# Twenty-one small loads, read by nobody, beside the K and V loads of a one-token attention kernel

## The chip, the cores and the metric

The kernel runs on one core of a Trainium2 chip. The metric is the device time of one execution in microseconds. Several executions are timed and the median is taken; one more is recorded by the hardware profiler, and the traces are from that one. The engines of the core are TensorE (PE in the profile, PEld for its weight loads), VectorE (DVE), ScalarE (ACT), GpSimd (POOL) and SyncE (SP). SP does no arithmetic here: it issues DMAs. Sixteen DMA engines move the data between the chip's main memory (HBM) and the core's on-chip memory.

## The reference

One new token is decoded. Part A is attention of 32 query heads over a cache of 8 key/value heads, each with 32768 positions of 128 bf16 values. Part B is a gated feed-forward block of width 1792. A scalar gate mixes the two.

```
def _A_ref(x, k_cache, v_cache, wq, wo):
    q = (x @ wq) as [B, 32, Sq, 128];  k, v = each cache head repeated 4 times
    scores = einsum("bhqd,bhkd->bhqk", q, k) * (Dh ** -0.5)
    p = softmax(scores)
    o = einsum("bhqk,bhkd->bhqd", p, v)
    return o as [B, Sq, 4096] @ wo

def _B_ref(x, w_gate, w_up, w_down):
    return (silu(x @ w_gate) * (x @ w_up)) @ w_down

g = sigmoid((x * gate_w).sum(-1))
return g * A + (1 - g) * B
```

Here B = Sq = 1 and D = 512. The K and V caches hold 8 x 32768 x 128 bf16 values each, 134 MB together, out of 148 MB that the kernel reads.

## The kernel before, in words

The program is written engine by engine, with semaphores between the engines; the order on each engine is the order of the code, and there is no scheduler.

**The pages.** On-chip memory holds five pages (`page`, each 128 partitions x 32 KB, 4.2 MB), called A, B, C, V and F in the code (PG_A to PG_F; the V loads use the last two). The K cache of one head takes two pages (A and B, or B and C, by turns), the V cache of one head the other two. So there is room for the K of one head, half of the next, and the V of one.

**SyncE's order** (lines 303 to 363, function `_(sp)`). It issues wq (line 340), w_gate and w_up (342), then the K loads of heads 0 and 1 in halves (320), and from head 2 on one load of 8.4 MB for each head (311). Between them stand the V loads (335): K of head g, then V of head g-1. A K load waits until PE has read half of the K pages of the head before (`sem_fill`), a V load until PE is done with the V pages of the head before (`sem_v_free`). The last V load goes into the K pages. Behind them come w_down (350, tile `wd`, and 358 for its rest, which waits for a memset by GpSimd on line 301), and the output weights wo in five pieces (363). SyncE's DMAs go through one queue, q1 in the profile.

**PE** has a loop over the 8 heads. `emit_k` (lines 391 to 415) brings each K page into PSUM by transposes (line 371, tile `pst`), VectorE copies the result into on-chip memory (line 765, tile `ktT`), and PE multiplies it with the queries (line 383, `ps_sc`). Then the maximum is taken (420, 424), ScalarE computes the exponentials (633, tile `ET`), and `emit_v` multiplies them with the V pages of the head before (line 440, `ps_o`). After the loop come the last head's V, w_down, and wo (lines 235 and 246).

**GpSimd** (lines 276 to 301) makes a few constants, and then relays the arrival of the K pages. PE waits on two semaphores for the two halves of a head's K. For heads 0 and 1 two DMAs raise them; from head 2 on one DMA raises only the first, `sem_k[0]`. So GpSimd waits for it and raises the second:

```
                for g in range(1, G):
                    pool.wait_ge(sem_k[1], 16 * g)
                    if g > 1:
                        pool.wait_ge(sem_k[0], 16 * (g + 1))
                    else:
                        pool.wait_ge(sem_k1, 16)
                    pool.sem_inc(sem_k[1], 16)
```

PE asks for the second semaphore before the second half of a head, after the eight transposes of the first half. GpSimd issues no DMA in this version. The kernel's end is the store of the output in two halves, issued by SyncE and ScalarE (line 270); SyncE then waits for both (line 822).

Of the kernel before, what the change touches and what calls it, by code (L numbers as in the profile page):

```python
# [8 lines left out]
BF16 = mybir.dt.bfloat16  # L9
# [3 lines left out]
def bass_gated_mix__gqa_block_cached__swiglu_ffn__decode_kernel(  # L13
# [61 lines left out]
    NPG = 5  # L75
    assert G % 2 == 0
    PAD = 768

    XH, XE, XQ, FX = 2, 4, 4, 4
    XP = XE * XQ  # L80
# [6 lines left out]
    with ExitStack() as es:  # L87
        def S_(name):
            return es.enter_context(nc.semaphore(name))
# [10 lines left out]
        sem_ld_wd = S_("s_ld_wd")  # L100
        sem_ld_wx = S_("s_ld_wx")
        sem_wz = S_("s_wz")
        sem_ones = S_("s_ones")
        sem_dc = S_("s_dc")
        sem_pz = S_("s_pz")
# [42 lines left out]
        def T(name, shape, dt):  # L148
            return es.enter_context(nc.sbuf_tensor(name, shape, dt))
# [18 lines left out]
        tX = T("tX", [XS, FX], BF16)  # L168
        pad = T("pad", [128, PAD // 2], BF16)
        page = T("page", [128, NPG, PAGE], BF16)  # L170
# [14 lines left out]
        O2a = T("O2a", [128, WOJ], BF16)  # L185
        O2 = T("O2", [128, WOJ], BF16)
        res_row = T("res_row", [128, 128], BF16)

        def P(name, shape, dt):
            return es.enter_context(nc.psum_tensor(name, shape, dt))  # L190
# [78 lines left out]
        def emit_store(eng, half, rows):  # L269
            eng.dma_start(  # L270
                out[0, 0, 256 * half : 256 * (half + 1)].rearrange("(c n) -> c n", c=2),
                rows[31 + 64 * half : 33 + 64 * half, :],
            ).then_inc(sem_out, 16)

        with nc.Block("main") as block:
            @block.gpsimd
            def _(pool):
                pool.memset(ones_f[:, :], 1.0).then_inc(sem_ones, 1)
                pool.memset(ones_bf[:, :], 1.0).then_inc(sem_ones, 1)
                pool.memset(r_row[:, 0, 0:1], 0.0).then_inc(sem_r, 1)  # L280
                n, k = 1, 1
                while n < 128:
                    pool.wait_ge(sem_r, k)
                    pool.tensor_scalar(
                        r_row[:, 0, n : 2 * n], r_row[:, 0, 0:n], float(n), None, op0=ALU.add
                    ).then_inc(sem_r, 1)
                    n *= 2
                    k += 1
                pool.wait_ge(sem_r, k)
                pool.tensor_scalar(  # L290
                    r_row[:, 1, :], r_row[:, 0, :], -1.0, None, op0=ALU.mult
                ).then_inc(sem_r, 1)
                for g in range(1, G):
                    pool.wait_ge(sem_k[1], 16 * g)
                    if g > 1:
                        pool.wait_ge(sem_k[0], 16 * (g + 1))
# [3 lines that stand above are left out]
                pool.wait_ge(sem_fill, UPG * G)  # L300
                pool.memset(wz, 0.0).then_inc(sem_wz, 1)  # L301

            @block.sync
            def _(sp):
                def load_k(g):
                    lo = PG_A if g % 2 else PG_B
                    dst = page[:, lo : lo + NB, :].rearrange("p b (r d) -> p b r d", d=DH)
                    src = A_k_cache[0, g, :, :].rearrange("(p b r) d -> p b r d", b=NB, r=R)
                    if g > 1:
                        sp.wait_ge(sem_fill, UPG * (g - 1) + UPP)  # L310
                        sp.dma_start(
                            dst.rearrange("p b r d -> p (b r d)"),
                            src.rearrange("p b r d -> p (b r d)"),
                        ).then_inc(sem_k[0], 16)
                        return
                    for b in range(NB):
                        first = lo + b == PG_B
                        if g and first:
                            sp.wait_ge(sem_fill, UPP)
                        sp.dma_start(dst[:, b, :, :], src[:, b, :, :]).then_inc(  # L320
                            sem_k[0] if first else sem_k1 if g else sem_k[1], 16
                        )

                def load_v(g):
                    src = A_v_cache[0, g, :, :].rearrange("(p b r) d -> p b r d", b=NB, r=R)
                    if g == G - 1:
                        lo, sem = PG_L, sem_vl
                        sp.wait_ge(sem_fill, UPG * g + UPP)
                    else:
                        lo, sem = PG_V, sem_v  # L330
                        if g:
                            sp.wait_ge(sem_v_free, STEP * (g + 1))
                        else:
                            sp.wait_ge(sem_pe_h, 1)
                    sp.dma_start(
                        page[:, lo : lo + NB, :].rearrange("p b n -> p (b n)"),
                        src.rearrange("p b r d -> p (b r d)"),
                    ).then_inc(sem, 16)

                sp.dma_start(wq_v, A_wq.rearrange("(p c) n -> p c n", c=KC)).then_inc(sem_q, 16)  # L340
                for w, src in enumerate((B_w_gate, B_w_up)):
                    sp.dma_start(
                        wgu[:, w, :, :], src.rearrange("(p c) f -> p c f", c=KC)
                    ).then_inc(sem_f, 16)
                load_k(0)
                for g in range(1, G):
                    load_k(g)
                    load_v(g - 1)
                load_v(G - 1)
                sp.dma_start(  # L350
                    wd[:, :, :], B_w_down[0:FR, :].rearrange("(p j) n -> p j n", j=FM)
                ).then_inc(sem_ld_wd, 16)
                sp.wait_ge(sem_wz, 1)
                rest = B_w_down[FR:F, :].rearrange(
                    "(h q e i) n -> h e q (i n)", h=XH, q=XQ, e=XE
                )
                for h in range(XH):
                    sp.dma_start(wx[h], rest[h]).then_inc(sem_ld_wx, 16)
                sp.wait_ge(sem_v_free, STEP * G)
                src = A_wo.rearrange("(p j) n -> p j n", j=WOJ)  # L360
                for k, s in enumerate(sem_wo):
                    a, b = WO_CUTS[k], WO_CUTS[k + 1]
                    sp.dma_start(wo_v[:, a:b, :], src[:, a:b, :]).then_inc(s, 16)  # L363
# [445 lines left out]
        pe, act, dve, sp = nc.tensor, nc.scalar, nc.vector, nc.sync  # L809
# [9 lines left out]
        for half, eng in enumerate((sp, act)):  # L819
            eng.wait_ge(sem_dve_row, 1)  # L820
            emit_store(eng, half, res_row)
        sp.wait_ge(sem_out, 32)


# [26 lines left out]
```

## Time and profile before

| | |
|---|---|
| median of 3 runs | 349.11 us (349.1 to 349.25) |
| profiled execution, its own time | 349.16 us |
| span of its trace, first to last instruction | 347.8 us |
| mean granted clock of TensorE | 0.851 of full speed |
| read from HBM | 148.11 MB, 426 GB/s over the span |

How to read the views: times are microseconds from the span's start, unless marked ns. L371 is line 371 of the kernel. A tile's name followed by an arrow shows what is written from what. In a list of waits the columns are: who waited, for whom, microseconds in total, how often, the longest. In a timeline or a chain they are: start, duration, what. A DMA instruction on "SPq" shows the time that SyncE needs to issue it, and not the transfer. A large load is many packets, spread over the 16 DMA engines; when an engine has done its part of a load, it writes its count to a semaphore, a packet of 4 bytes. The answers on DMA packets count the packets that start in the window which the text names; "under 2 KB" includes those under 512 B.

### The profile page before, as it was taken

To read this page: it belongs to the slowest core of one execution; us is meant where nothing else is said; L and a number is where in the kernel's file an instruction comes from. 1 tells how busy PE (TensorE), PEld (TensorE's weight loads), DVE (VectorE), ACT (ScalarE), POOL (GpSimd) and SP (SyncE) were. 2 spreads that over 40 slices of the span, in tenths; PEclk is the share of its full clock that TensorE was granted. 3 is DMA by queue.
4 is the path that set the end of the run, shared out by engine and by line. 5 is a ranking of instruction groups with operands and counts; after the bars stand their busy time and mean duration, and the time that the engine had idled before them with its cause. 6 is when DMAs were issued, how large, how long until landed. Compare 5 with 4: busy or idle time off the path is not lost.

```text
span 347.8 us, 8869 instructions
## 1 busy us (share of the span) xinstructions
PE 260.8 (75%) x3925; PEld 220.6 (63%) x3925; DVE 186.6 (54%) x232; ACT 33.4 (10%) x143; POOL 4.6 (1%) x16
## 2 busy tenths in 40 slices
PE   1354995999749982999459982999469972999475
PEld 1124994998449941997259942996269842996232
DVE  3144995698119931697129921895149820895101
ACT  1002000300130003000300003000400012000400
POOL 3000000000000000000000000000000000002000
PEclk9996999699659987699959985898869985898669
DMA  8999999999999999999999999999999999999996
GB/s 322 419 459 426 420 422 458 469 414 437 414 430 475 415 437 415 437 467 415 437 407 445 467 414 437 407 452 460 414 437 407 452 460 415 437 407 452 406 418 261
DMA packets 3946, 148.21 MB, mean 426 GB/s; under 512 B 450, under 2 KB 580, under 8 KB 868
## 3 DMA queue, kind: packets, MB, share of 16 engines
q1 hardware_dynamic: 3932, 148.11, 98.7%
q8 instruction: 6, 0.10, 0.1%
q10 hardware_dynamic: 8, 0.00, 0.0%
HBM read 148.11 MB, written 0.00 MB: 426 GB/s over the span
## 4 chain that ended last, share of the span: by engine, by line
DMA 64%; PE 33%; DVE 2%; issue 1%; SPq 1%; ACT 0%; DVEq 0%
DMA page<-in_A_k_cache_dram 52%; PE pst L371 24%; DMA page<-in_B_w_up_dram 6%; DMA page<-in_A_wo_dram 6%; PE ps_sc L383 5%; PE ps_o L440 2%; PE pst L535 1%; DVE ktT L722 1%; DVE ktT L765 0%; SPq L363 0%; PE ps_m L553 0%; PE ps_m L566 0%; DVE ktT L712 0%; DVE ktT L710 0%; PE ps_sc L246 0%
## 5 line engine op out<-in xcount | busy, mean ns | idle before, releaser
L765 DVE COPY ktT<-pst 128x2048 bf16<-128x2048 bf16 x128 | 153.3, 1221 | 64.6 <-PE pst L371 60.4
L371 PE MATMUL pst<-ident_f,page 128*128 128x128 f32 x1024 | 147.2, 299 | 39.5 <-DMA page<-in_A_k_cache_dram 38.2
L371 PEld LDWEIGHTS pst<-ident_f,page 128*128 128x128 f32 x1024 | 126.0, 154 | 43.9 <-DMA page<-in_A_k_cache_dram 38.8
L383 PE MATMUL ps_sc<-qcur,ktT 128*128 128x8 bf16 x2048 | 64.1, 166 | 6.3 <-DVE ktT L765 6.3
L383 PEld LDWEIGHTS ps_sc<-qcur,ktT 128*128 128x128 bf16 x2048 | 63.8, 97 | 8.0 <-DVE ktT L765 7.1
L440 PE MATMUL ps_o<-page,ET 128*16 128x512 bf16 x512 | 39.4, 477 | 5.5 <-DMA page<-in_A_v_cache_dram 5.5
L440 PEld LDWEIGHTS ps_o<-page,ET 128*16 128x16 bf16 x512 | 15.0, 107 | 26.1 <-issue 18.8
L633 ACT ACTIVATE ET<-ps_sc,nbias 128x128 bf16 x64 | 23.9, 555 | 49.9 <-DVE nbias L791 49.9
L626 ACT ACTIVATE acc<-ps_o 128x512 f32<-128x512 f32 x8 | 4.8, 597 | 223.8 <-PE ps_o L440 218.9
L783 DVE TENSOR_REDUCE gm<-ps_m 4x1 f32<-4x128 f32 x8 | 2.2, 279 | 40.6 <-PE ps_m L420 40.6
L633 ACT ACTIVATION_READ_ACCUMULATOR ET<-ps_sc,nbias 128x1 f32 x64 | 18.3, 285 | 0.0
L773 DVE TENSOR_REDUCE pmaxf<-ps_sc 128x4 f32<-128x512 f32 x16 | 11.0, 686 | 8.4 <-PE ps_sc L383 8.4
L497 PE MATMUL pst<-page,xT 128*1 128x512 bf16 x32 | 3.6, 627 | 8.9 <-DMA page<-in_A_wq_dram 8.9
L461 PE MATMUL ps_m<-sel,acc 128*128 128x4 f32 x64 | 8.4, 255 | 1.8 <-ACT acc L626 1.6
L461 PEld LDWEIGHTS ps_m<-sel,acc 128*128 128x128 f32 x64 | 7.7, 191 | 2.5 <-ACT acc L626 2.2
L424 PE MATMUL ps_m<-diag,ones_f 4*128 4x4 f32 x16 | 3.8, 306 | 6.8 <-DVE diag L787 6.8
L424 PEld LDWEIGHTS ps_m<-diag,ones_f 4*128 4x128 f32 x16 | 3.3, 259 | 8.4 <-issue 8.4
L750 DVE RECIPROCAL rS<-ps_m 128x4 f32<-128x4 f32 x9 | 1.6, 182 | 12.2 <-PE ps_m L461 12.2
L497 PEld LDWEIGHTS pst<-page,xT 128*1 128x1 bf16 x32 | 0.9, 115 | 10.7 <-issue 10.7
L685 DVE CAST ktT<-pst 128x1024 bf16<-128x1024 f32 x2 | 2.4, 1220 | 8.2 <-PE pst L497 8.2
L452 PEld LDWEIGHTS ps_m<-esum,ones_f 128*128 128x128 f32 x32 | 4.2, 190 | 3.5 <-issue 3.5
L301 POOL MEMSET page<- 48x2048 bf16 x1 | 1.8, 1798 | 311.7 <-PE pst L371 311.7
(76 smaller groups left out, 54.6 us busy)
## 6 DMA issues: line engine op xcount, KB each, us to landing
page<-in_A_k_cache_dram SPq DMA_DIRECT2D x4, 4096.0 KB, 34.9
page<-in_A_wq_dram SPq DMA_DIRECT2D x1, 4096.0 KB, 13.4
page<-in_A_wo_dram SPq DMA_DIRECT2D x1, 2048.0 KB, 17.4
page<-in_B_w_gate_dram SPq DMA_DIRECT2D x1, 1792.0 KB, 17.2
page<-in_B_w_up_dram SPq DMA_DIRECT2D x1, 1792.0 KB, 21.0
wd<-in_B_w_down_dram SPq DMA_DIRECT2D x1, 1664.0 KB, 30.3
page<-in_A_wo_dram SPq DMA_DIRECT2D x1, 1152.0 KB, 19.8
page<-in_A_wo_dram SPq DMA_DIRECT2D x1, 512.0 KB, 20.6
```

Of the source, the lines that this page charges most:

```text
L371: ins = pe.transpose(pst[u % NST][:, k * 128 : (k + 1) * 128], kv[:, n * 128 : (n + 1) * 128], ident_f[:, :],)
L383: ins = pe.matmul(ps_sc[b][:, col : col + 2 * HPG], kt[:, k, e, :], qcur[:, e, :], start=(e == 0), stop=(e == 1),)
L424: pe.matmul(ps_m[:, M_B0 : M_B0 + HPG], ones_f[0:HPG, :], diag[:, :], start=True, stop=True,).then_inc(sem_b, STEP)
L440: ins = pe.matmul(ps_o[32 * c : 32 * c + RQ * HPG, :], ET[:, n : n + RQ, :].rearrange("p n h -> p (n h)"), v[:, k * RQ : (k + 1) * RQ, :], ...
L452: pe.matmul(ps_m[:, M_S0 : M_S0 + HPG], ones_f[:, :], esum[:, b, :], start=(b == 0), stop=(b == NB - 1),)
L461: ins = pe.matmul(ps_m[:, M_P0 : M_P0 + HPG], acc[:, q, :], sel4[:, q * HPG : (q + 1) * HPG], start=(q == 0), stop=(q == RQ - 1),)
L497: ins = pe.matmul(pst[0][32 * k : 32 * k + 1, t * QN : (t + 1) * QN], xT[:, c : c + 1], wq_v[:, c, n : n + QN], start=(c == 0), stop=(c == ...
L535: ins = pe.matmul(pst[1][32 * k : 32 * k + 1, w * 512 : w * 512 + FS], xT[:, c : c + 1], wgu[:, w, c, k * FS : (k + 1) * FS], start=(c == ...
L626: act.activation(part, ps_o[:, :], ACT.Copy).then_inc(sem_acc, STEP)
L633: act.activation(ET[:, b * R : (b + 1) * R, h], sc[:, h, bass.ds(bank, R)], ACT.Exp, bias=nbias[:, h : h + 1], scale=SCALE, accum_out=esum ...
L765: dve.tensor_copy(ktT[:, n % NKT, :], pst[n % NST][:, :].bitcast(BF16)).then_inc(sem_cp, 1)
L773: dve.tensor_reduce(pmaxf[:, b, :], sc, AX.X, ALU.max).then_inc(sem_d, 1)
```

## The change

SyncE issues 15 additional loads (`load_mark`): one after each K load from head 1 on, and one after each V load. The first has 15 rows, the next 14, and so on down to one; a row is 128 bytes (64 bf16 values) of wq. GpSimd issues six loads just before it waits for the K pages of head 4: of 1, 1, 3, 5, 7 and 15 rows, with row lengths from 160 to 352 bytes. The tiles that they fill, `mark` and `turn0` to `turn5`, are read by nobody. At the end SyncE waits for both groups, ahead of the wait for the output's store. On each engine the other instructions stay as they were, in the same order.

```
--- before.py
+++ after.py
@@ -75,6 +75,8 @@
     PAD = 768
+    MARKS = list(range(15, 0, -1))
+    TURNS = [(1, 80), (1, 96), (3, 112), (5, 144), (7, 160), (15, 176)]
 
@@ -185,6 +189,8 @@
         res_row = T("res_row", [128, 128], BF16)
+        mark = T("mark", [16, len(MARKS), 64], BF16)
+        turn_t = [T(f"turn{i}", [16, n], BF16) for i, (_, n) in enumerate(TURNS)]
 
@@ -291,6 +297,9 @@
                 for g in range(1, G):
+                    if g == 4:
+                        for t, (k, n) in zip(turn_t, TURNS):
+                            pool.dma_start(t[0:k, :], A_wq[0:k, 0:n]).then_inc(sem_turn, 16)
                     pool.wait_ge(sem_k[1], 16 * g)
@@ -337,6 +346,13 @@
+                marks = list(enumerate(MARKS))
+
+                def load_mark():
+                    if marks:
+                        m, n = marks.pop(0)
+                        sp.dma_start(mark[0:n, m, :], A_wq[0:n, 0:64]).then_inc(sem_mark, 16)
+
@@ -345,8 +361,12 @@
                 for g in range(1, G):
                     load_k(g)
+                    load_mark()
                     load_v(g - 1)
+                    load_mark()
                 load_v(G - 1)
+                load_mark()
+                assert not marks
                 sp.dma_start(
@@ -819,6 +839,8 @@
             emit_store(eng, half, res_row)
+        sp.wait_ge(sem_mark, 16 * len(MARKS))
+        sp.wait_ge(sem_turn, 16 * len(TURNS))
         sp.wait_ge(sem_out, 32)
```

The two new semaphores, `sem_mark` and `sem_turn`, are made beside the others.

More of the change, by code (lines that the diff above doesn't have):

```diff
@@ L102, in bass_gated_mix__gqa_block_cached__swiglu_ffn__decode_kernel @@
         sem_wz = S_("s_wz")
+        sem_mark = S_("s_mark")
+        sem_turn = S_("s_turn")
         sem_ones = S_("s_ones")
```

## The prediction

> **What bounds the kernel now.** I began with the head of the page, the busy shares in slices and the table of the queues.
>
> ```profile
> span 347.8 us, 8869 instructions
> ...
> PE 260.8 (75%) x3925; PEld 220.6 (63%) x3925; DVE 186.6 (54%) x232; ACT 33.4 (10%) x143; POOL 4.6 (1%) x16
> ...
> DMA  8999999999999999999999999999999999999996
> ...
> q1 hardware_dynamic: 3932, 148.11, 98.7%
> q8 instruction: 6, 0.10, 0.1%
> ```
>
> The row of digits is the mean busy share of the 16 DMA engines: nine tenths or more in every slice but the first and the last. Nearly all of it is one queue, q1, SyncE's. PE is busy for 75% of the span and DVE for 54%, so neither of them is the bound as a whole. Next I read one long stretch with the view by windows (the columns end in DMA share and GB/s), and then the waits of PE.
>
> ```profile
> 48.00:320.00 272.00, 217.77 (x3366) 191.94 (x3368) 159.94 (x185) 24.55 (x118) 1.80 (x1) 0.85 1.00 434
> ```
>
> ```profile
> PE pst L371 <- DMA page<-in_A_k_cache_dram: 38.2, 7, 7.9
> ```
>
> In the 272 us between 48 and 320 the DMA share is 1.00 at 434 GB/s, or 27.1 GB/s for each engine. No engine pauses between one load and the next. PE waits for the K pages seven times, 38.2 us in all, and this is its longest wait by far. So the time is the number of bytes over the rate of the engines, plus a short start and a short end. A change pays or costs here if it makes an engine's queue run dry, if it adds to an engine's work, or if it makes the end longer.
>
> The issue times of the SyncE queue tell whether a queue can run dry. First the timeline of that engine, then its waits, then the median time from issue to landing.
>
> ```profile
> 43.95 0.33 SPq L320 DMA_DIRECT2D page<-in_A_k_cache_dram  x1
> 44.32 0.43 SPq L335 DMA_DIRECT2D page<-in_A_v_cache_dram  x1
> ```
>
> ```profile
> 73.44 0.33 SPq L311 DMA_DIRECT2D page<-in_A_k_cache_dram  x1
> 91.53 0.33 SPq L335 DMA_DIRECT2D page<-in_A_v_cache_dram  x1
> ...
> 305.73 0.43 SPq L350 DMA_DIRECT2D wd<-in_B_w_down_dram  x1
> 317.52 1.48 SPq L358 DMA_DIRECT2D page<-in_B_w_down_dram  x2
> ```
>
> ```profile
> SPq L311 <- PE pst L371: 130.6, 6, 28.7
> SPq L335 <- PE ps_o L440: 103.1, 6, 17.7
> ...
> SPq L335 <- PE pst L371: 22.8, 1, 22.8
> ```
>
> ```profile
> page<-in_A_v_cache_dram SPq DMA_DIRECT2D x8, 28.4
> ```
>
> A V load is 8.39 MB (8 heads of 32768 x 128 bf16, one head each). At 434 GB/s it streams for 19.3 us, but it lands 28.4 us after its issue. So it stands some 9 us in the queue behind the load before it. SyncE itself idles: it waits 130.6 us ahead of six K loads 103.1 us ahead of six V loads and 22.8 us ahead of the last V load.
>
> Last, what the engines look like at one landing. The K load issued at 189.38 lands near 216. These are three answers on the DMA packets, for 213.9 to 214.7, 214.7 to 215.3 and 215.3 to 216.0 us.
>
> ```profile
> DMA packets 20, 0.66 MB, mean 819 GB/s; under 512 B 10, under 2 KB 10, under 8 KB 10
> ```
>
> ```profile
> DMA packets 0, 0.00 MB, mean 0 GB/s; under 512 B 0, under 2 KB 0, under 8 KB 0
> ```
>
> ```profile
> DMA packets 12, 0.39 MB, mean 562 GB/s; under 512 B 6, under 2 KB 6, under 8 KB 6
> ```
>
> Loads are made of large packets, so the packets under 512 B are the closing semaphore writes, one for each engine: 10 + 0 + 6 = 16. Ten engines finish their share, then nothing closes for 0.6 us, then the other six finish. The engines run side by side without waiting for each other, and **the six late engines set each landing**. Up to 0.6 us of extra work on any of the ten early ones is free.
>
> **The change, part by part.** It removes nothing and moves nothing between engines: the instructions of PE, DVE and ACT are the same in both programs. SyncE gets 15 more DMA instructions, GpSimd six, and SyncE two more waits at its end.
>
> *Issue time on SyncE.* The prices are in the view by tile (columns: ns least, median, most).
>
> ```profile
> L335 SPq DMA_DIRECT2D page<-in_A_v_cache_dram x8: 327/328/432, 44.3 to 305.4; - x8
> L358 SPq DMA_DIRECT2D page<-in_B_w_down_dram x2: 641/712/784, 317.5 to 318.4; - x2
> ```
>
> A mark of few rows can be like either, so 15 marks take 15 x 0.33 = 4.9 us to 15 x 0.78 = 11.8 us of SyncE's time. I take 0.33, since a mark has a plain shape. Thirteen of them stand where SyncE then waits for PE for many microseconds, in the waits quoted above, and cost nothing. Two have an instruction right behind them that waits for nothing: the V load at 44.32 goes out at 44.7 to 45.1, and the wd load at 305.73 at 306.1 to 306.5. Both stand in the queue behind the rest of a load that was just issued (4.2 MB of K or 8.4 MB of V, 10 to 19 us of streaming), so neither is late. What comes after wd is held by GpSimd's memset until 317.52 anyway. Without that cover each would cost its 0.33 to 0.78 us.
>
> *Work on the DMA engines.* All marks go into SyncE's queue between the large loads, so each of their packets takes time on an engine that has no pause. The price of a small packet comes from the end of the kernel, where the last loads have short rows. This is the answer for 344.5 to 345.5 us.
>
> ```profile
> DMA packets 150, 0.18 MB, mean 184 GB/s; under 512 B 20, under 2 KB 100, under 8 KB 150
> ...
> q1 hardware_dynamic: 150, 0.18, 50.4%
> ```
>
> 50.4% of 16 engines in 1 us is 8.06 us of engine time. The 0.18 MB at 27.1 GB/s are 6.6 us. The other 1.4 us over 150 packets is about 10 ns for each packet, whatever its size (8 to 11 with the rounding of 0.18). A row of 128 B is then 10 + 4.7 = 15 ns and the semaphore write behind it 10 ns: 25 ns for each mark on each engine that it uses. The marks have 15 + 14 + ... + 1 = 120 rows, so an engine has 7.5 of them on average, at least 0 and at most 15: 0.19 us, between 0 and 0.37 us. An early engine hides even 0.37 us in its 0.6 us. No trace row tells which engines are the late ones, so I take the average for them.
>
> The Trainium skill, "DMA: Bandwidth & Descriptors", section "Why a DMA increments its semaphore by 16 and not by 1", says that a load of n rows from SyncE uses the largest divisor up to 16, and the lowest-numbered engines. By that page the lowest engine has all 15 marks and the highest none, and the sum would be 0.37 or 0 in place of 0.19; no view here numbers the engines.
>
> *GpSimd's six loads.* In the changed program the first two rows are cut into 16 pieces each, so there are 16 + 16 + 3 + 5 + 7 + 15 = 62 data packets, and up to 6 x 16 = 96 semaphore writes. 158 x 10 ns, and 10 KB at 27.1 GB/s (0.4 us), are 2.0 us over 16 engines: 0.12 us each. GpSimd's own time for them is in no trace of before. From below it is nothing. From above, its longest instruction is 1.80 us (the one in the row by windows), and six of those are 10.8 us. I take about 1 us each, for no sum depends on it: between the relay for head 3 and the need of the one for head 4 there is time, as these rows of the chain of waits show.
>
> ```profile
> 138.93 5.38 PE pst L371 x24
> ...
> 177.56 5.23 PE pst L371 x24
> ...
> 189.38 26.77 DMA page<-in_A_k_cache_dram
> ```
>
> PE begins on the K pages of head 3 at 138.93, and GpSimd can start its DMAs then. PE begins on head 4 at 177.56 and needs GpSimd's relay only for the second half of it, at about 189.4. That is 50 us of cover for 0 to 10.8 us.
>
> *The end.* The two waits are passed long before: the marks are complete when the wd load behind them is. They run beside the output's store.
>
> ```profile
> SPq L822 <- DMA out_dram<-res_row: 1.0, 1, 1.0
> ```
>
> **Sum:** 0.19 + 0.12 = 0.31 us more on the late engines, between 0 and 0.5. The profiled execution took 349.16 us (its span of 347.8 and 1.4 around it), which gives 349.47. The median of the runs is 349.11, and from there it is 349.42. I forecast **349.4 us**, 0.1% more. A measurement of this kernel can tell about 0.2%, 0.7 us, from no change, so this counts as the same. A gain has no source in the sum, as no engine gets less to do.
>
> **The rivals.**
>
> *A small load leaves a hole (slower).* The engine might pause until a mark's row is in, ahead of the next load's first packet. The least a small DMA takes from issue to landing is the 1.0 us of the store above. With 15 holes of 1.0 us on a late engine that is 15 us: 364. Against it stands the DMA share of 1.00 at all borders between loads; for it, that none of those borders has a packet of 128 B read between two large ones. It decides from 0.7 us on: 47 ns for each mark on an engine with 15, or 93 ns with 7.5. A mild hole of 0.1 us on 7.5 marks beside the sum gives 350.2. Chance 0.12, most of it below 351.
>
> The same page of the Trainium skill, section "Anatomy of one DMA — SWDGE (gpsimd) path", puts about 2 us of fixed cost on each DMA. By that figure 15 marks one after the other would be an estimated 30 us. The share of 1.00 speaks against paying it in a row.
>
> *GpSimd's relay comes late (slower).* Lines 293 to 299 forward the arrival of K pages. If the six DMAs hold GpSimd for more than 50 us, over 8.4 us each, PE starts the second half of head 4 late. The loads have about 9 us of cover more, so 10 us each, 60 in all, would be 1 us past both covers: 350.4. Nothing in the profile is near 8 us on GpSimd. Chance 0.02.
>
> The Trainium skill, "SBUF — State Buffer", section on the "DVE blocks DMA" trap, says that GpSimd cannot write its descriptors while some VectorE copies run. [...]
>
> *Another block of code is fetched (slower).* Queue q8 above is code: 6 packets of 16 KB, 0.1% of 16 x 347.8 us = 5.6 us, 0.9 us of one engine each. Six fetches and six late engines: a fetch seems to be what makes an engine late. If the added instructions bring one more and it falls on a late engine, that is 349.4 + 0.9 = 350.3. On an early engine it is largely hidden. 21 instructions are few beside 16 KB. Chance 0.08.
>
> *The late engines come out less late (faster).* A fetch that falls elsewhere changes who is last. At most the 0.6 us gap and some 0.3 go: 348.4. Nothing in the change aims there. Chance 0.03.
>
> That the loads are left out of the program is excluded: all 21 are in the instruction lists of the changed one.
>
> **How the numbers follow.** Forecast 0.75, holes 0.12, code 0.08, relay 0.02, less late 0.03. Faster by over 0.2% is 0.03, slower by over 0.2% is 0.12 + 0.08 + 0.02 = 0.22, the rest is 0.75. The forecast's own range is 349.0 to 349.7: its sum of 0 to 0.5 on 349.1, and the spread of the runs. With the fetch and the milder half of the holes, the range that holds 8 in 10 is 349.0 to 350.4.
>
> **What would show it.** The DMA share between 48 and 320 us stays at 1.00 and the K loads keep their period of some 38.6 us (138.93 to 177.56). SyncE's queue shows each mark at some 0.3 us and the V load of 44.32 some 0.4 us later, its landing unchanged. The gap between the two groups of engines stays, shifted by tenths. It is wrong if slices of the DMA row fall below 9, if queue q8 has more than 6 packets, or if PE waits for GpSimd ahead of L371.

## The result, and the profile after

The changed kernel takes 350.41 us (median of 5, 350.33 to 350.5) against 349.11 before: a ratio of 1.0036 with the interval 1.0021 to 1.005. It is 1.3 us slower, more than the 0.3 us of the forecast: 0.7 us above the forecast's own range (up to 349.7), and 0.01 us past the upper end of the range that was to hold 8 in 10 (350.4).

The page of the profile after, in the rows that bear on the prediction:

```profile
span 349.1 us, 8891 instructions
...
DMA  8999999999999999999999999999999999999995
...
DMA packets 4378, 148.24 MB, mean 425 GB/s; under 512 B 882, under 2 KB 1012, under 8 KB 1300
...
q1 hardware_dynamic: 4172, 148.13, 98.5%
q8 instruction: 6, 0.10, 0.1%
q0 software_dynamic: 192, 0.01, 0.0%
```

In the DMA row the first slice is 8 as before, the last is 5 where it was 6, and no slice between them has fallen below 9. The code queue q8 still has six packets, so no code was fetched anew. q1 has 4172 - 3932 = 240 packets more: 120 rows and 120 closing writes, so a mark of n rows used n engines. The new queue q0 is GpSimd's; its data is 10 KB. Its 192 packets are 62 of data, as the prediction had them, and 130 writes of 4 bytes, where it had up to 96.

Now the instructions that were added, in the timeline of SyncE and in that of GpSimd (start, duration, what).

```profile
45.47 0.48 SPq L354 DMA_DIRECT2D mark<-in_A_wq_dram  x1
46.00 0.35 SPq L344 DMA_DIRECT2D page<-in_A_v_cache_dram  x1
46.39 1.19 SPq L354 DMA_DIRECT2D mark<-in_A_wq_dram  x1
73.66 0.33 SPq L320 DMA_DIRECT2D page<-in_A_k_cache_dram  x1
...
306.04 0.29 SPq L354 DMA_DIRECT2D mark<-in_A_wq_dram  x1
306.37 0.33 SPq L370 DMA_DIRECT2D wd<-in_B_w_down_dram  x1
317.82 1.43 SPq L378 DMA_DIRECT2D page<-in_B_w_down_dram  x2
```

```profile
139.62 3.19 POOL L302 DMA_DIRECT2D turn<-in_A_wq_dram  x6 [135.60 <-POOLq L308]
```

SyncE issues a mark in 0.29 to 0.48 us, and one in 1.19, behind which it waits for PE anyway. GpSimd issues its six loads in 3.19 us, long before its relay is needed at 189.

Where does the time go, then? The chain of waits shows when PE starts on a head's K pages, that is, when they have landed.

```profile
100.33 4.38 PE pst L391 x24
111.35 27.61 DMA page<-in_A_k_cache_dram
139.01 5.31 PE pst L391 x24
150.92 27.50 DMA page<-in_A_k_cache_dram
189.66 27.43 DMA page<-in_A_k_cache_dram
217.14 5.38 PE pst L391 x24
...
255.79 4.96 PE pst L391 x24
...
324.98 21.79 DMA page<-in_A_wo_dram
...
347.42 0.29 DVE res_row L838
```

The same rows of before have these times:

```profile
100.32 4.61 PE pst L371 x24
...
138.93 5.38 PE pst L371 x24
...
151.10 26.42 DMA page<-in_A_k_cache_dram
...
216.20 4.70 PE pst L371 x24
...
254.84 4.38 PE pst L371 x24
...
346.19 0.29 DVE res_row L818
```

At 139 the two kernels are level (0.08 us apart). The K load of head 4 then lands 0.90 us late: 150.92 + 27.50 = 178.42, against 151.10 + 26.42 = 177.52. At 217 the changed kernel is 0.94 us late, at 255 still 0.95. So in this execution nearly all of the loss arises in one period, between the landings at 139 and 178, although marks are issued from 45 to 306 us. It is the period in which GpSimd's loads are under way; the last of them lands near 170 us. At the end the loss has grown to 1.23: the output's copy on VectorE starts at 347.42 instead of 346.19.

In that stretch the engines are nearly as busy as ever, but on longer packets. The answer on DMA packets for 143.9 to 146.3 us, first before, then after:

```profile
DMA packets 16, 1.05 MB, mean 437 GB/s; under 512 B 0, under 2 KB 0, under 8 KB 0
...
q1 hardware_dynamic: 16, 1.05, 100.9%
```

```profile
DMA packets 31, 0.98 MB, mean 410 GB/s; under 512 B 16, under 2 KB 16, under 8 KB 16
...
q1 hardware_dynamic: 15, 0.98, 100.2%
q0 software_dynamic: 16, 0.00, 0.4%
```

Before, 16 packets of 64 KB take 100.9% of 16 engines x 2.4 us: 2.42 us each. After, 15 take 100.2% of the same: 2.57 us each. The small packets of q0 take 0.4%, and the large ones beside them have become 6% longer in this window. (Whether 15 or 16 start in it depends in part on where it cuts; the duration of each does not.) **The share counts a held-up packet as busy**; the bytes and the duration of the large packets tell.

Each packet of the trace has a start and a duration, and sums over all of them give the whole account. After, the large packets took 0.36 us more on each engine than before. There are also real pauses, moments in which an engine has no packet: 4.3 us of engine time, 0.27 us for each engine; the trace before has none between 20 and 330 us. Most of them, 4.1 us, lie between 140 and 160 us; at 157 us five of the 16 engines stand still for 0.3 us. The additional small packets are 0.2 to 0.3 us for each engine. The three make 0.83 to 0.93, and near 306 us the large packets start 0.88 us later than before, on average over the engines. What is missing up to 1.25 is in the section on the prediction.

### The profile page after: what moved, and what is told of

Same layout as the page of the kernel before. It is cut to its first block, busy times and chain, and to the rows that moved or that the text cites. A ratio compares the mean times of both kernels' runs of the same rounds, so it can differ in the third digit from the quotient of the medians.

```text
span 349.1 us, 8891 instructions
## 1 busy us (share of the span) xinstructions
PE 258.4 (74%) x3925; PEld 218.8 (63%) x3925; DVE 186.5 (53%) x232; ACT 33.4 (10%) x143; POOL 7.8 (2%) x22
## 3 DMA queue, kind: packets, MB, share of 16 engines
q1 hardware_dynamic: 4172, 148.13, 98.5%
## 4 chain that ended last, share of the span: by engine, by line
DMA 59%; PE 34%; DVE 3%; issue 2%; SPq 1%; ACT 0%; DVEq 0%
DMA page<-in_A_k_cache_dram 47%; PE pst L391 25%; DMA page<-in_A_wo_dram 6%; PE ps_sc L403 6%; DMA page<-in_B_w_up_dram 6%; DVE ktT L785 2%; PE ps_o L460 1%; PE pst L555 1%; DVE ktT L742 1%; SPq L383 0%; PE ps_m L573 0%; PE ps_m L586 0%; DVE pmaxf L793 0%; DVE ktT L732 0%; DVE ktT L730 0%
## 5 line engine op out<-in xcount | busy, mean ns | idle before, releaser
L391 PE MATMUL pst<-ident_f,page 128*128 128x128 f32 x1024 | 146.6, 298 | 42.2 <-DMA page<-in_A_k_cache_dram 40.5
L391 PEld LDWEIGHTS pst<-ident_f,page 128*128 128x128 f32 x1024 | 125.5, 154 | 46.6 <-DMA page<-in_A_k_cache_dram 41.1
L460 PE MATMUL ps_o<-page,ET 128*16 128x512 bf16 x512 | 38.2, 465 | 6.4 <-DMA page<-in_A_v_cache_dram 6.4
L460 PEld LDWEIGHTS ps_o<-page,ET 128*16 128x16 bf16 x512 | 14.2, 105 | 26.6 <-issue 18.8
L302 POOL DMA_DIRECT2D turn<-in_A_wq_dram x6 | 3.2, 538 | 135.6 <-POOLq L308 135.6
```

The source lines that it names most:

```text
L391: ins = pe.transpose(pst[u % NST][:, k * 128 : (k + 1) * 128], kv[:, n * 128 : (n + 1) * 128], ident_f[:, :],)
L460: ins = pe.matmul(ps_o[32 * c : 32 * c + RQ * HPG, :], ET[:, n : n + RQ, :].rearrange("p n h -> p (n h)"), v[:, k * RQ : (k + 1) * RQ, :], ...
```

## The experiments

Three theories stood at the start. G: GpSimd's loads cost most of the 1.3 us. M: the marks leave holes at the borders between loads. X: only the two together cost. All kernels are compared with before on the same chip, where it took 349.2. The intervals reach some 0.3 us to each side, so an addition of 0.2 to 0.3 us is not clear of noise by itself.

The edits are against the changed kernel, and only their main lines are shown. A group that is left out loses its wait at the end as well. The two kernels with GpSimd's loads moved (turns_by_sync, turns_spread) have no marks. All kernels named after marks have no loads from GpSimd, and those named marks_16 with an addition have the edit of marks_16 too.

**The marks alone.**

```
-    TURNS = [(1, 80), (1, 96), (3, 112), (5, 144), (7, 160), (15, 176)]
+    TURNS = []
```

> SyncE's 15 marks alone, without GpSimd's six loads. Theory G (GpSimd's loads cost most of the 1.3 us, by stretched packets and pauses between 139 and 180 us): the marks cost about 15 ns each on an engine, up to 15 of them on the lowest engines, so +0.2 to +0.35 us, near 349.4. Theory M (the marks leave holes at the borders between loads): nearly all of the 1.3 us stays, near 350.2. Theory X (only marks and GpSimd's loads together cost): near 349.4 here, and little in turns_only too.

It took 349.64, ratio 1.0013 (1.0004 to 1.0022): +0.44 us. That is neither M's 350.2 nor the bare 0.2 to 0.35, though the interval includes the latter. At the landing of head 3's K, 136.5 to 139 us, before had this:

```profile
DMA packets 32, 1.05 MB, mean 419 GB/s; under 512 B 16, under 2 KB 16, under 8 KB 16
...
q1 hardware_dynamic: 32, 1.05, 97.1%
```

and the marks alone this:

```profile
DMA packets 54, 1.05 MB, mean 420 GB/s; under 512 B 38, under 2 KB 38, under 8 KB 38
...
q1 hardware_dynamic: 54, 1.05, 99.9%
```

There are 16 large packets in both. 2.8% of 40 us of engine time are 1.1 us; the 22 additional small packets explain 0.2 of it at 10 ns each. The large packets behind a mark became some 0.06 us longer each.

**GpSimd's loads alone.**

```
-    MARKS = list(range(15, 0, -1))
+    MARKS = []
```

> GpSimd's six loads alone, without the marks. Theory G: +0.8 to +1.1 us, near 350.1, with the large packets of all engines stretched between 139 and 180 us. Theory M: +0.1 us, 349.2. Theory X: +0.1 to +0.5 us, 349.2 to 349.6.

349.43, ratio 1.0008 (0.9999 to 1.0017): +0.23 us, not clear of no change. G, which needed +0.8 at least, is refuted. Alone, the two parts sum to 0.67, half of the loss; X can only hold for the other half.

**The same six loads from SyncE.**

```
+                    if g == 4:
+                        for t, (k, n) in zip(turn_t, TURNS):
+                            sp.dma_start(t[0:k, :], A_wq[0:k, 0:n]).then_inc(sem_turn, 16)
```

> The same six small loads of 1, 1, 3, 5, 7 and 15 rows, issued by SyncE behind the K load of head 4 in place of GpSimd, no marks. If the path through GpSimd's own queue makes the cost (theory G), SyncE's queue carries them for some 15 ns per packet: +0.0 to +0.2 us, 349.1 to 349.3. If small packets of these sizes cost by themselves, +0.8 us or more as in turns_only.

349.7, ratio 1.0015 (1.0006 to 1.0024), with executions from 349.17 to 350.37. GpSimd's path is not what makes them dear: six loads of 32 rows in all, in one place of SyncE's queue, do not cost less, and by chance between nothing and over 1 us. The place is not the same: they stand behind the K load of head 4, which lands near 178 us, and GpSimd's own loads ran before that.

**GpSimd's loads one at a time.**

```
-                    if g == 4:
-                        for t, (k, n) in zip(turn_t, TURNS):
-                            pool.dma_start(t[0:k, :], A_wq[0:k, 0:n]).then_inc(sem_turn, 16)
+                    if g > 1:
+                        t, (k, n) = turn_t[g - 2], TURNS[g - 2]
+                        pool.dma_start(t[0:k, :], A_wq[0:k, 0:n]).then_inc(sem_turn, 16)
```

> GpSimd's six loads alone, one for each of heads 2 to 7 in place of six in a row. If each of GpSimd's loads has its price for itself, the sum is that of turns_only (near 350.1). If the price comes from six of them crowding the same engines at once, or from their meeting with one border between loads, it falls to a third or less: 349.2 to 349.4.

349.24, ratio 1.0003 (0.9994 to 1.0012). Spread over the heads 2 to 7 they cost nothing that can be measured.

**The change again.** No edit.

> The changed kernel once more, beside the three others of this call on their chip. If marks (+0.44) and GpSimd's loads (+0.23) simply add, it takes 349.2 + 0.67 = 349.9; if they raise each other's price, it repeats its 1.3 us: 350.4 to 350.5.

350.44, ratio 1.0037 (1.0024 to 1.0051), on another chip than the two parts alone. The 1.25 us are firm, and they are nearly twice the sum of the parts. Where they arise is not: in this trace PE starts on heads 3, 4 and 5 at 139.56, 178.47 and 217.14, so 0.63 us are lost before 139 already, 0.28 between there and 178, and next to nothing behind it.

**Another order of heads.**

```
-                    src = A_k_cache[0, g, :, :].rearrange("(p b r) d -> p b r d", b=NB, r=R)
+                    src = A_k_cache[0, (g + 4) % G, :, :].rearrange("(p b r) d -> p b r d", b=NB, r=R)
```

and the same for V.

> The 15 marks alone, with the K and V caches of heads 4, 5, 6, 7, 0, 1, 2, 3 loaded in this order (the queries then meet the cache of other heads; work and times are the same). In marks_only the large packets were longer than 2.418 us only just behind the landings at 117, 137, 156, 176 and 195 us. If the place in HBM makes them so (heads 1 to 4 of V, 3 to 5 of K), these packets move to the ends of the execution (20 to 60 and beyond 270 us). If it is the time in the execution, they stay at 117 to 195. Time near 349.6 by both.

349.7, ratio 1.0014 (1.0005 to 1.0023), but the profiled execution was the fastest of eleven (349.18), and its large packets were not longer anywhere. So this run answers nothing on place or time. It does show that the delay comes and goes between executions.

**Sixteen rows in each mark.**

```
-    MARKS = list(range(15, 0, -1))
+    MARKS = [16] * 15
```

> 15 marks of 16 rows each, so every engine has 15 of them, in place of 15 to none. If a mark costs its own packets, 15 ns, and nothing else, every engine ends 0.23 us later: 349.4. If uneven marks (some engines without) make the longer packets, these are gone and it is 349.4 as well, with the sum of the stretches near before's 0.4 us over 16 engines. If any small packet at a border makes them, the stretches are 4.5 us or more again and the time 349.6 to 349.8.

350.1, ratio 1.0028 (1.0017 to 1.0038), no execution below 349.96: +0.9 us, of which the packets themselves are some 0.25 (marks_16_close below). More rows, more delay, and it isn't the unevenness of the marks. This is the kernel to experiment on, since it has the effect each time.

**No marks in the middle.**

```
+                        if not 3 <= m <= 7:
```

> The marks without the five behind V of head 1, K of head 3, V of head 2, K of head 4 and V of head 3, at whose landings the longer packets were. If those five marks made them, the stretches fall from 4.9 to under 1 us over 16 engines and the time to 349.3 to 349.4 (ten marks at 15 ns, 0.15 us). If the stretches come from the engines' being out of step since the first mark, they stay, and the time is 349.6.

349.36, ratio 1.0004 (0.9995 to 1.0013): +0.16, about the price of ten marks' own packets; in its trace the large packets are no longer than in before. The five marks in the middle carried the rest of marks_only.

**Sixteen rows, another order of heads.** The edits of the two kernels above together.

> marks_16 with the heads' caches loaded in the order 4, 5, 6, 7, 0, 1, 2, 3 (the queries meet the cache of other heads). In marks_16 the loads between 60 and 200 us came late (heads 2 to 5 of K, 1 and 2 of V), those behind 215 us did not. If the place in HBM decides, the late periods move to heads 2 to 5's new places, to the last loads from 240 us on and the first ones. If the time in the execution decides, they stay between 60 and 200 us. Time 350.1 by both.

350.18, ratio 1.0031 (1.0019 to 1.0043). The starts of PE on the heads, first in marks_16, then with the heads moved:

```profile
100.26 5.38 PE pst L391 x24
...
139.19 4.85 PE pst L391 x24
...
178.03 4.38 PE pst L391 x24
...
216.90 5.24 PE pst L391 x24
...
255.55 4.70 PE pst L391 x24
...
294.24 5.38 PE pst L391 x24
```

```profile
139.34 5.38 PE pst L391 x24
...
178.08 4.88 PE pst L391 x24
...
217.01 4.38 PE pst L391 x24
...
255.65 5.34 PE pst L391 x24
...
294.35 4.77 PE pst L391 x24
```

The periods are 38.93, 38.84, 38.87 up to 217, then 38.65 and 38.69. With the heads moved they are 38.74 and 38.93 up to 217, then 38.64 and 38.70. Bare marks would make 38.64 (before's) + 0.03. In both the loss is over at 217. It goes by the place in the execution, not by the place of K and V in HBM.

**Sixteen rows that lie together.**

```
-                        sp.dma_start(mark[0:n, m, :], A_wq[0:n, 0:64]).then_inc(sem_mark, 16)
+                        src = A_wq[0:1, 0 : 64 * n].rearrange("o (r w) -> (o r) w", w=64)
+                        sp.dma_start(mark[0:n, m, :], src).then_inc(sem_mark, 16)
```

> marks_16 with the 16 rows of 128 bytes read from 2 KB in a row in place of rows 8 KB apart. If the reads of rows 8 KB apart hold up each other or the large reads in HBM, the extra over the bare 0.23 us falls from some 0.6 to under 0.2: 349.4 to 349.6. If the reading side doesn't matter, 350.1 stays.

349.44, ratio 1.0008 (0.9999 to 1.0017). At +0.25 this is about the bare price. As many DMAs, rows, bytes and engines, the same tile, and 0.66 us less, only because the 16 rows are read from 2 KB in a row and not 8 KB apart. The packets behind the first landing with the delay, 78.2 to 80.4 us, in marks_16 and then here:

```profile
DMA packets 61, 0.99 MB, mean 448 GB/s; under 512 B 46, under 2 KB 46, under 8 KB 46
...
q1 hardware_dynamic: 61, 0.99, 108.9%
```

```profile
DMA packets 60, 0.99 MB, mean 448 GB/s; under 512 B 45, under 2 KB 45, under 8 KB 45
...
q1 hardware_dynamic: 60, 0.99, 104.4%
```

Both have 15 large packets. Of 35.2 us of engine time the first has 38.3 and the second 36.7 in packets (they run on past the window). Without 0.5 us of small packets that is 2.52 us for each large packet against 2.42.

**Sixteen rows, other partitions.**

```
-                        sp.dma_start(mark[0:n, m, :], A_wq[0:n, 0:64]).then_inc(sem_mark, 16)
+                        sp.dma_start(mark[0 : 8 * n : 8, m, :], A_wq[0:n, 0:64]).then_inc(sem_mark, 16)
```

> marks_16 with the 16 rows written to partitions 0, 8, 16, ... 120 in place of 0 to 15. If the writing of all engines into the same few partitions, beside the large writes there, makes the delay, the extra falls from some 0.6 to under 0.3: 349.4 to 349.7. If the writing side doesn't matter, 350.1 stays.

350.28, ratio 1.0033 (1.0021 to 1.0044), as slow as marks_16. So to write the rows to other partitions doesn't help, and the kernel before this one shows that to read them elsewhere does: the delay is on the reading side.

**The change without the marks in the middle.** The edit of marks_outside in the changed kernel.

> The changed kernel (marks and GpSimd's six loads) without the five marks between 110 and 200 us. marks_outside took +0.16 and turns_only +0.23. If marks and GpSimd's loads raise each other's price only where they meet between 110 and 200 us, this is the sum: 349.5 to 349.6. If GpSimd's loads make all marks dearer, 350.0 or more.

349.86, ratio 1.0018 (1.0009 to 1.0027). The five marks are worth 0.58 us here and 0.28 without GpSimd's loads, so the two do raise each other's price in the middle. But 0.67 is still more than 0.16 + 0.23. In its trace PE starts on heads 3, 4 and 5 like this:

```profile
138.82 4.38 PE pst L392 x24
...
177.74 5.21 PE pst L392 x24
...
216.38 4.67 PE pst L392 x24
```

The first period, with GpSimd's loads and no mark in it, is 38.92 us, the next 38.64. In turns_only the first is 38.68 (138.88 to 177.56). These are one execution each, but they agree with the times: marks that have passed before seem to make GpSimd's loads dearer.

## Why the prediction was wrong, step by step

It forecast 349.4, no change that can be measured, and the kernel is 0.36% slower. The bound was right: the kernel lives by the DMA engines, and what was added to them came out at the end. The price of the additions was wrong.

*Right.* The issue time on SyncE is hidden. The V load went out at 46.00 instead of 44.32, more than the 0.4 us of the text, because the K load ahead of it and its mark came later as well; head 2 still started at 100.33 against 100.32. GpSimd took 0.5 us for each load and its relay was in time. No block of code came. The end after VectorE's copy took 1.7 us, as before 1.6.

*Right as far as it went.* The price of a mark's own packets: 15 marks on every engine cost 0.25 us in marks_16_close, 17 ns for each mark with its closing write, against 25 in the text.

*The step that failed:* "A row of 128 B is then 10 + 4.7 = 15 ns and the semaphore write behind it 10 ns: 25 ns for each mark on each engine that it uses." It took a small read's price to be its own duration, and so did the 10 ns for each of GpSimd's packets. The runs put a second term beside it: the large reads behind it become longer, 2.52 us for 2.42 in marks_16, when the small rows lie 8 KB apart. In the changed kernel the 0.31 us of the sum became, as an average over the engines, 0.2 to 0.3 for the small packets, 0.36 for longer large packets and 0.27 for pauses. That the reading is what matters is shown for the marks; for GpSimd's rows it is an inference. The price was taken from wo's short packets at the end. By the code these lie 32 KB apart, but nothing large stands behind them; no row of before had a small read among large ones.

*The rival with the holes* named part of the event: the pauses are there, but the longer packets cost more. Its mild case, 0.1 us on 7.5 marks, gave 350.2, but it had a chance of 0.12. What spoke against it was "the DMA share of 1.00 at all borders between loads". That was weak evidence twice: none of those borders had a small read, as the text says itself, and the share cannot show such a delay. It stays at 1.00 while the packets get longer, and 0.27 us of pauses in 272 us are lost in its rounding. The estimate of 30 us beside this rival is made with a figure for loads that GpSimd issues; the marks are SyncE's, and 15 of them cost 0.25 us in marks_16_close. That the rival with the late relay gave 350.4 is luck: PE never waits for GpSimd ahead of L391.

*The signs.* None of the three that were to show the prediction wrong came; they had the same blind spot. But two that were to show it right failed. The K loads were to keep their period of some 38.6 us, and from 139.01 to 217.14 the two periods are 39.07 each on average. And the gap between the two groups of engines was to stay. At the landing near 216 us ten engines had closed by 214.56 and six from 215.44 on; after, five closed by 214.95 and eleven between 215.40 and 216.73. So the early engines did not hide what they got.

*The average* over the engines was a choice without a row, and the end, where 0.28 us were added beyond the 0.95, goes against it. In the page of before, 450 packets are under 512 B: 27 loads x 16 closing writes, 10 for the output and the two small inputs, and 8 that are left for the two loads of w_down's rest, so four engines each. The Trainium skill, "DMA: Bandwidth & Descriptors", section "Why a DMA increments its semaphore by 16 and not by 1", says that a load from SyncE uses the lowest-numbered engines. By that the same four would carry 15, 14, 13 and 12 of the marks. The counts of closing writes agree with its rule on how many engines. On which ones, the trace after agrees as far as it can, for it does not number them. From 230 us on each engine's packets follow each other without a gap, so that the 16 can be told apart by start and duration. The 4 KB packets of w_down's rest are then on just the four engines that have the most marks behind 230 us: 6, 5, 4 and 3. These four are the last to begin on wo, at 336.68 to 336.94 us, the other twelve by 336.62. In before the last of the 16 begins at 335.69. The difference is 1.25 us, as much as the whole loss.

**What stays open.** Why the reads that lie apart delay the others only until about 215 us (until 178 in both traces of the changed kernel); why marks raise the price of GpSimd's loads, it seems even of later ones; why engines pause in the changed kernel; whether GpSimd's rows, also 8 KB apart, would be free if they lay together. The last was not tried. The Trainium skill, the same page, section "Latency and other measured facts", tells of copies within HBM that slow down where rows lie a large power of two apart (207 GB/s at 512 KiB, 164 at 2 MiB, 103 at 4 MiB), and infers, without having verified it, that they meet in one channel of HBM. The 8 KB here are far below its range, so it does not cover this case, and no run here shows a channel.

## What to carry to other kernels

A small load in a queue that is always full can cost more than its own packets if its rows lie far apart (8 KB here): take the bytes from one stretch, or place the load outside of the streaming, which was not tried here. A DMA share of 1.00 does not show that the engines run at full rate; compare bytes in equal windows, or the duration of the large packets, before calling a queue undisturbed. And measure two additions together as well as apart: here the parts gave 0.67 us and the whole 1.25.

## What the runs showed of the hardware that I had not expected

- The packets of GpSimd's queue are taken between those of the large load, at first one by one: in the window from 143.9 to 146.3 us 16 of them stand beside 15 large ones. Its six loads were issued within 3.2 us, but in the view by tile they landed 9.0, 17.4 and 28.0 us (least, median, most) after their issue.

```profile
DMA to landing us min/median/max: 9.0/17.4/28.0
```

- The same kernel can have the delay or not: six small loads in one place of SyncE's queue gave 349.17 to 350.37 us in eleven executions.
